# Eight decoded weight pieces and a gate table: their stores moved from SyncE's queue to GpSimd's

## The chip, the core and the metric

The program runs on one core of a Trainium2 chip. The metric is the time of one execution on the device in microseconds (us), the median of the executions shown. Three executions of the kernel before took 786.92, 788.0 and 788.8 us, so the median is 788.0 us. One more execution was profiled; all rows below are of that one.

## The reference

Three layers follow one another on 2304 tokens of width 512.

```
scores = scale * q @ k^T            # 4 batches, 8 heads, 576 positions, head width 64
attn   = softmax(where(mask, scores + bias, -1e9))     # causal, window 128, linear bias
x      = attn @ v                   # 2304 x 512
expert = argmax(x @ w_gate); gate = softmax(x @ w_gate)[expert]
out[t] = gate[t] * relu(x[t] @ w1[expert]) @ w2[expert]   # 8 experts, 512 -> 1024 -> 512
y      = relu(out @ w_in)**2 @ w_out                       # 512 -> 2048 -> 512
```

`w_in` and `w_out` reach the kernel as 64-bit words (two 32-bit words for each number), so they have to be decoded to 32-bit floats on the chip before they can be used. All large products are done on 16-bit floats with a high and a low half for each number, three products in place of one.

## The kernel before, in words

The program is one long, unrolled stream. A framework orders the instructions of every engine and adds the waits; each engine then runs its own instructions strictly in that order. The queue that an instruction stands in therefore matters twice: for what it waits for, and for what waits behind it.

**Stages.** Attention runs to about 160 us and writes its result, split into halves, to DRAM (`xd`, line 415, issued by GpSimd). The eight experts follow, to about 425 us, each in two steps: `s1` (lines 804 to 814: 96 matmuls into PSUM, a RELU on ScalarE at line 813, the low half on VectorE at line 814) and `s2` (lines 855 to 869: 96 matmuls, a copy on ScalarE at line 867). The last layer runs from about 438 us on (`wide1`, `wide2`).

**Expert weights.** `load_w` (line 761) loads a piece of 512 KB from DRAM through SyncE's queue (line 770) into a ring `rw` of four buffers, and splits it into halves on ScalarE (line 784) and VectorE (line 785). The buffer is free when line 785 is done.

**Expert inputs.** `gather` (line 997) fetches rows of `xd` with indirect DMAs from GpSimd's queue (line 793) into a ring `xg` of six buffers. A gather has to wait until TensorE has transposed what was in its buffer (line 801, `turn`), and while it waits, GpSimd's queue stands still.

**Weights of the last layer.** While the experts run, `wide()` (line 939) is called now and then and does one piece. `out_step` (line 920) takes one of the sixteen 128-row pieces of `w_out`. It loads 512 KB into the same ring `rw` (line 879), and three VectorE instructions decode it into the lower half of one tile `dec` (lines 884, 885, 886). Its `finish` (line 925), which the next `wide()` calls, splits it into halves on ScalarE (line 930) and VectorE (line 931). Eight of the sixteen pieces (`SENT`) are not kept on the chip: their halves go into the upper half of `dec`, and from there to DRAM (`wod`, 256 KB each, line 934). Since `dec` is one tile, line 930 of the next piece may not write before the store of this one has landed. Those eight are the first eight steps; the sixteen steps of `w_in` (`in_step`, line 889) follow, whose decoding uses the upper half of `dec` as well; `fetch_out` (line 970) brings `wod` back just before the last layer.

The store itself isn't issued by `finish`. It is put on a list (`self.stored`), and the next call of `wide()` issues it on SyncE's queue ahead of its own work, or after it when the next step is one of `w_in`.

**The gate table.** `gates()` (line 576) computes the gate of each token, transposes it into `gt` (line 596), and stores it to DRAM (`gd`) with eight small DMAs from SyncE's queue: four of 2 KB (line 600) and four of 0.25 KB (line 603). It is read again by indirect DMAs of GpSimd (line 757) from 284 us on.

In the rows below, the eight stores of `w_out` pieces are called p1 to p8 in the order of their issue.

Of the kernel before, what the change touches and what calls it, by code (L numbers as in the profile page):

```python
# [22 lines left out]
N, DM, E, F, F2 = 2304, 512, 8, 1024, 2048  # L23
P = 128
# [65 lines left out]
class K:  # L90
# [485 lines left out]
    def gates(self):  # L576

        nc, cp, V = self.nc, self.cp, self.nc.vector
        sh = [P, NT, E]
        G = cp.tile(sh, F32, name="G2")  # L580
        V.tensor_tensor(G, self.lg, self.mx[:, :, 0:1].to_broadcast(sh), op=ALU.subtract)
        nc.scalar.activation(G, G, AF.Exp, scale=1.0 / (XSC * GSC))
        gs = cp.tile([P, NT], F32, name="gs")
        V.tensor_reduce(gs, G, axis=AX.X, op=ALU.add)
        V.tensor_scalar(gs, gs, 1e-9, XSC * W1SC * W2SC, op0=ALU.add, op1=ALU.mult)

        self.gate = cp.tile([P, NT], F32, name="gate")
        g3 = gs.rearrange("p (g t) -> p g t", g=2)
        for g in range(2):
            V.reciprocal(self.gate[:, 8 * g:8 * g + 8].rearrange("p (b u) -> p b u", b=2),  # L590
                         g3[:, g, :8].rearrange("p (u b) -> p b u", b=2))
        V.reciprocal(self.gate[:, 16:], g3[:, :, 8])
        gp = self.psum("d", [P, P])[:NT]
        nc.tensor.transpose(gp, self.gate, self.idf)
        gt = cp.tile([NT, P], F32, name="gateT")
        V.tensor_copy(gt, gp)

        gd = self.gd.rearrange("(a r) o -> a (r o)", a=B)
        for a in range(B):
            nc.sync.dma_start(gd[a, :512].rearrange("(u p) -> u p", p=P), gt[4 * a:4 * a + 4])  # L600
        for a in range(B):
            o = a % 2 * 64
            nc.sync.dma_start(gd[a:a + 1, 512:], gt[16 + a // 2:17 + a // 2, o:o + 64])

    def order(self):

# [313 lines left out]
    def out_step(self, fc):  # L920

        nc = self.nc
        f = self.wide_load(self.wo, [(slice(fc * P, (fc + 1) * P), lambda r, k: r, DM, lambda st, k: st)])

        def finish():
            if fc in KEPT:
                dst = self.wo_s[fc]
            else:
                dst = self.dec[:, 512:].bitcast(F16).rearrange("p (a d) -> p a d", a=2)
            nc.scalar.activation(dst[:, 0], f, AF.Copy, scale=WOSC)  # L930
            nc.vector.scalar_tensor_tensor(dst[:, 1], f, WOSC, dst[:, 0], op0=ALU.mult, op1=ALU.subtract)  # L931
            if fc not in KEPT:
                o = SENT.index(fc) * 2 * DM
                self.stored.append(lambda: nc.sync.dma_start(self.wod[:, o:o + 2 * DM],
                                                             dst.rearrange("p a d -> p (a d)")))

        return finish

    def wide(self, k=1):
        def store():  # L940
            while self.stored:
                self.stored.pop()()

        for _ in range(k):
            store()
            if self.finish:
                self.finish()
                self.finish = None
            if self.steps:
                f, *a = self.steps.pop(0)  # L950
                if f == self.in_step:
                    store()
                self.finish = f(*a)

    def open_wide(self, stack):
        wp = self.wp = stack.enter_context(self.tc.tile_pool(name="wp", bufs=1))
        self.wi_s = [wp.tile([P, 2, 2, 7 * P], F16, name=f"wi{k}", tag=f"wi{k}") for k in range(8)]
        self.wo_s = {}
        self.stored, self.finish = [], None
        self.steps = [(self.out_step, fc) for fc in SENT] + \  # L960
            [(self.in_step, fp, kp) for fp in range(8) for kp in range(2)] + [(self.out_step, fc) for fc in KEPT]

# [13 lines left out]
    def experts(self, stack):  # L976
# [33 lines left out]
        gather(1)  # L1010
        self.places()
        wide(2)
        self.s2([w[2, 0, k] for k in range(4)], self.hte, 0, EB * P, lambda d: wide())
        xt = self.new_xf(P)
        self.transpose_whole(xgs[0][0], xt)
        self.offsets()
        for e in range(E):
# [13 lines left out]
            for fc in range(8):  # L1031
                ht = self.hts(e, W)[fc]
                if e == 0:
                    self.s1_whole(fc, w[1, e, fc // 2], xt, ht, W)
                else:
                    self.s1(fc, w[1, e, fc // 2], xt[:, :, :W], ht, W)
                hts.append(ht)
                if fc % 2 == 1 and more and e > 0:
                    w[1, e + 1, fc // 2] = self.load_w(1, e + 1, fc // 2)
                if fc in STEPS[e][0]:  # L1040
                    wide()
                if fc in (3, 5, 7) and more:
                    turn(nxt, e + 1, fc // 2 - 1)
                if e == 7 and fc == 1:
                    next(nrm)
                next(table, None) if table else None
# [283 lines left out]
```

## Time and profile before

| | |
|---|---|
| median of three executions | 788.0 us (786.92 to 788.8) |
| the profiled execution's own time | 787.16 us |
| its span, first to last instruction | 785.5 us |
| TensorE busy | 731.0 us (93%) |
| VectorE, ScalarE, GpSimd busy | 539.7, 362.6, 158.2 us |
| moved by SyncE's queue, by GpSimd's | 75.70 MB, 14.63 MB |

The span is 1.7 us shorter than the execution's own time, which holds what lies around the program. A busy share over the whole span hides that the stages differ: the last layer, from 440 us on, is nearly pure matmul work, and what idle time TensorE has lies before it. Rows of a timeline give start and duration in us, then engine, line, operation and tiles; in square brackets stands how long the engine was idle before the instruction and what ended that. SyncE's DMA instructions are issues: the transfer itself goes on after them, up to its landing.

### The profile page before, as it was taken

How to read it: one execution, taken by the hardware profiler on the slowest of the kernel's cores; microseconds unless marked ns; L12 is line 12 of the kernel's file. 1: busy time of each engine (PE TensorE's matmuls, PEld its weight loads, DVE VectorE, ACT ScalarE, POOL GpSimd, SP SyncE). 2: the span in 40 equal slices, each digit the busy share in tenths (PEclk: the TensorE clock that was granted, in tenths of full speed). 3: DMA queues.
4: the chain of work that ended last, by engine and by line, in shares of the span. 5: the costliest groups of instructions: out<-in, count | busy, mean ns of one | idle time of the engine just before them, and what ended most of it. 6: DMA issues, size and time to landing. Idle time of an engine off the chain costs nothing. (4 is left out here: it accounts for less than half of the span.)

```text
span 785.5 us, 18379 instructions
## 1 busy us (share of the span) xinstructions
PE 731.0 (93%) x7546; PEld 562.5 (72%) x7546; DVE 539.7 (69%) x1361; ACT 362.6 (46%) x637; POOL 158.2 (20%) x167
## 2 busy tenths in 40 slices
PE   6999999898878988998898999999999999999996
PEld 5889899687544654677698677777777777777772
DVE  5888888755679977878887865656656565657440
ACT  5888888634356554655643323232323232323220
POOL 4573212445101877100000000000000000000000
PEclk9999999998999999999999999999999999999999
DMA  9896307756686676765722200000000000000000
GB/s 335 299 359 142 98 29 211 207 121 204 215 248 219 195 222 202 239 199 180 252 82 61 78 15 14 15 15 15 15 15 15 15 15 14 16 3 27 2 28 28
DMA packets 36431, 91.54 MB, mean 117 GB/s; under 512 B 5992, under 2 KB 14200, under 8 KB 36344
## 3 DMA queue, kind: packets, MB, share of 16 engines
q1 hardware_dynamic: 29816, 75.70, 30.5%
q0 software_dynamic: 6528, 14.63, 5.9%
q8 instruction: 61, 1.00, 0.6%
q14 instruction: 26, 0.21, 0.1%
HBM read 77.44 MB, written 12.94 MB: 115 GB/s over the span
## 5 line engine op out<-in xcount | busy, mean ns | idle before, releaser
L1177 PEld LDWEIGHTS <-wi 128*128 128x128 f16 x3024 | 172.0, 98 | 4.0
L1238 POOL DMA_INDIRECT out_dram<-o,oid x18 | 17.5, 973 | 447.0 <-ACT o L1236 447.0
L1197 ACT CAST wr<-work 128x1024 f16<-128x1024 f32 x36 | 37.6, 1045 | 123.1 <-DVE work L1196 123.1
L784 ACT ACTIVATE wr<-rw 128x1024 f16<-128x1024 f32 x60 | 62.6, 1055 | 51.6 <-DMA rw<-in_w_dram 50.6
L785 DVE SCALAR_TENSOR_TENSOR wr<-rw,wr 128x1024 f16<-128x1024 f32 x60 | 72.6, 1219 | 18.7 <-ACT wr L784 18.6
L864 PE MATMUL ps_c<-work,wr 128*128 128x352 f16 (+5 forms) x256 | 72.8, 291 | 8.6 <-ACT yT L867 5.1
L865 PE MATMUL ps_c<-work,wr 128*128 128x352 f16 (+5 forms) x256 | 72.9, 291 | 8.2 <-DVE work L814 8.2
L866 PE MATMUL ps_c<-work,wr 128*128 128x352 f16 (+5 forms) x256 | 72.8, 291 | 0.0
L305 PE MATMUL ps_a<-yT,wr 128*128 128x192 f32 (+2 forms) x288 | 64.6, 345 | 6.2 <-DMA wr<-in_q_dram 4.5
L1202 DVE TENSOR_TENSOR work<-work 128x512 f32<-128x512 f32 x18 | 12.4, 691 | 77.5 <-ACT work L1189 77.5
L1177 PE MATMUL ps_a<-work,wi 128*128 128x128 f16 x1032 | 64.6, 219 | 0.0
L1177 PE MATMUL ps_c<-work,wi 128*128 128x128 f16 x1008 | 64.3, 221 | 0.0
L1177 PE MATMUL ps_b<-work,wi 128*128 128x128 f16 x984 | 62.1, 220 | 0.0
L317 ACT ACTIVATE pb<-pb,nm 128x192 f32<-128x192 f32 (+2 forms) x144 | 55.8, 432 | 12.0 <-DVE nm L310 11.8
L1229 PE MATMUL ps_d<-wr 128*128 128x512 f16 x144 | 54.6, 379 | 2.7 <-PEq L1076 2.7
L1230 PE MATMUL ps_d<-wr 128*128 128x512 f16 x144 | 54.6, 379 | 0.0
L1231 PE MATMUL ps_d<-wr 128*128 128x512 f16 x144 | 54.6, 379 | 0.0
L1231 PE MATMUL ps_d<-rw,wr 128*128 128x512 f16 x144 | 54.6, 379 | 0.0
L1230 PE MATMUL ps_d<-rw,wr 128*128 128x512 f16 x144 | 54.6, 379 | 0.0
L1229 PE MATMUL ps_d<-rw,wr 128*128 128x512 f16 x144 | 54.6, 379 | 0.0
L1231 PEld LDWEIGHTS <-wr 128*128 128x128 f16 x288 | 28.2, 98 | 33.9
L1229 PEld LDWEIGHTS <-wr 128*128 128x128 f16 x288 | 28.1, 98 | 33.3 <-issue 2.9
(261 smaller groups left out, 1691.5 us busy)
## 6 DMA issues: line engine op xcount, KB each, us to landing
rw<-in_w_dram SPq DMA_DIRECT2D x60, 512.0 KB, 5.1
rw<-in_wo_dram SPq DMA_DIRECT2D x16, 512.0 KB, 5.5
rw<-in_wi_dram SPq DMA_DIRECT2D x32, 256.0 KB, 4.1
wr<-in_q_dram SPq DMA_DIRECT2D x14, 512.0 KB, 18.1
xd<-xhl POOLq DMA_DIRECT2D x16, 256.0 KB, 6.6
yT<-in_k_dram SPq DMA_DIRECT2D x7, 576.0 KB, 7.6
rw<-in_v_dram SPq DMA_DIRECT2D x12, 325.0 KB, 5.6
wr<-in_q_dram SPq DMA_DIRECT2D x8, 256.0 KB, 6.5
```

The source lines that it names most:

```text
L305: nc.tensor.matmul(ps[:, s, first:hi], q[g, u, hh // 4][:, hh % 4, s if u < 4 else 0, :], self.kt[g, hh // 2][:, hh % 2, key0:key0 + hi - ...
L317: self.last_exp = nc.scalar.activation(pb[:, s, first:hi], pb[:, s, first:hi], AF.Exp, bias=nm[:, s:s + 1], scale=-1.0)
L784: self.nc.scalar.activation(t[:, 0], st, AF.Copy, scale=sc)
L785: self.nc.vector.scalar_tensor_tensor(t[:, 1], st, sc, t[:, 0], op0=ALU.mult, op1=ALU.subtract)
L864: nc.tensor.matmul(py, wh, hh, start=fc == 0, stop=False)
L865: nc.tensor.matmul(py, wh, hl, start=False, stop=False)
L866: nc.tensor.matmul(py, wl, hh, start=False, stop=fc == 7)
L1177: self.nc.tensor.matmul(ps[:, j], w[:, kp, a, w0 * P:(w0 + 1) * P], v[:, 2 * x + kp], start=kp + b == 0, stop=kp == 1 and b == 2)
L1197: nc.scalar.copy(g[0][:, :, i], ci)
L1229: nc.tensor.matmul(py, gh, wh, start=n == 0, stop=False)
L1230: nc.tensor.matmul(py, gh, wl, start=False, stop=False)
L1231: nc.tensor.matmul(py, gl, wh, start=False, stop=n == 15)
```

## The change

Both kinds of store are issued from GpSimd's queue, and that of a decoded piece at once in `finish`. The list of stores and the two places that emptied it are gone.

```diff
         gd = self.gd.rearrange("(a r) o -> a (r o)", a=B)
         for a in range(B):
-            nc.sync.dma_start(gd[a, :512].rearrange("(u p) -> u p", p=P), gt[4 * a:4 * a + 4])
+            nc.gpsimd.dma_start(gd[a, :512].rearrange("(u p) -> u p", p=P), gt[4 * a:4 * a + 4])
         for a in range(B):
             o = a % 2 * 64
-            nc.sync.dma_start(gd[a:a + 1, 512:], gt[16 + a // 2:17 + a // 2, o:o + 64])
+            nc.gpsimd.dma_start(gd[a:a + 1, 512:], gt[16 + a // 2:17 + a // 2, o:o + 64])
...
             if fc not in KEPT:
                 o = SENT.index(fc) * 2 * DM
-                self.stored.append(lambda: nc.sync.dma_start(self.wod[:, o:o + 2 * DM],
-                                                             dst.rearrange("p a d -> p (a d)")))
+                nc.gpsimd.dma_start(self.wod[:, o:o + 2 * DM], dst.rearrange("p a d -> p (a d)"))
...
     def wide(self, k=1):
-        def store():
-            while self.stored:
-                self.stored.pop()()
-
         for _ in range(k):
-            store()
             if self.finish:
                 self.finish()
                 self.finish = None
             if self.steps:
                 f, *a = self.steps.pop(0)
-                if f == self.in_step:
-                    store()
                 self.finish = f(*a)
...
-        self.stored, self.finish = [], None
+        self.finish = None
```

## Rows read from the trace of the kernel before

**Rows 1.** Busy time by stretch; columns: PE, PEld, DVE, ACT, POOL, PEclk, DMA share, GB/s

```profile
176.00:240.00 64.00, 50.66 (x397) 36.65 (x396) 39.84 (x68) 29.13 (x50) 15.78 (x19) 0.90 0.70 221
...
440.00:785.50 345.50, 339.22 (x3634) 237.09 (x3631) 199.30 (x295) 97.52 (x131) 17.51 (x18) 1.00 0.04 15
```

**Rows 2.** Waits of PE, 176 to 232 us: total, times, longest, in us

```profile
PE ps_c L865 <- DVE work L814: 3.3, 1, 3.3
...
PE ps_b L810 <- DVE work L814: 2.2, 1, 2.2
```

**Rows 3.** Timeline of DVE around 210 us

```profile
209.49 0.69 DVE L931 SCALAR_TENSOR_TENSOR dec<-dec 128x512 f16<-128x512 f32 x1
210.09 0.55 DVE L814 SCALAR_TENSOR_TENSOR work<-ps_b,work 128x384 f16<-128x384 f32 x1
```

**Rows 4.** Timeline of ACT, 187 to 216 us

```profile
187.97 0.63 ACT L930 ACTIVATE dec<-dec 128x512 f16<-128x512 f32 x1
...
193.57 0.63 ACT L930 ACTIVATE dec<-dec 128x512 f16<-128x512 f32 x1 [1.64 <-DMA wod<-dec]
...
200.18 0.63 ACT L930 ACTIVATE dec<-dec 128x512 f16<-128x512 f32 x1 [4.75 <-DMA wod<-dec]
...
203.80 0.63 ACT L930 ACTIVATE dec<-dec 128x512 f16<-128x512 f32 x1 [2.67 <-DMA wod<-dec]
...
207.26 1.06 ACT L784 ACTIVATE wr<-rw 128x1024 f16<-128x1024 f32 x1 [2.45 <-DMA rw<-in_w_dram]
...
208.59 0.62 ACT L930 ACTIVATE dec<-dec 128x512 f16<-128x512 f32 x1
...
215.98 0.61 ACT L930 ACTIVATE dec<-dec 128x512 f16<-128x512 f32 x1
```

**Rows 5.** Timeline of SyncE's queue, 183 to 211 us: p1 to p6 and one weight load

```profile
183.90 0.33 SPq L934 DMA_DIRECT2D wod<-dec  x1
...
189.35 0.33 SPq L934 DMA_DIRECT2D wod<-dec  x1
...
194.95 0.33 SPq L934 DMA_DIRECT2D wod<-dec  x1
...
201.56 0.33 SPq L934 DMA_DIRECT2D wod<-dec  x1
...
203.48 0.34 SPq L770 DMA_DIRECT2D rw<-in_w_dram  x1
...
205.19 0.35 SPq L934 DMA_DIRECT2D wod<-dec  x1
...
210.20 0.33 SPq L934 DMA_DIRECT2D wod<-dec  x1
```

**Rows 6.** The eight stores of line 934: duration of the issue (ns), and landing

```profile
L934 SPq DMA_DIRECT2D wod<-dec x8: 326/330/355, 183.9 to 223.9; - x8
...
DMA to landing us min/median/max: 2.1/3.7/5.4
```

**Rows 7.** Waits of SyncE's queue, 176 to 226 us: total, times, longest

```profile
SPq L934 <- DVE dec L931: 17.5, 7, 4.6
```

**Rows 8.** Line 415, two GpSimd stores at 141.9 and 142.5 us: landing

```profile
DMA to landing us min/median/max: 3.7/3.7/3.7
```

**Rows 9.** Line 793, nine GpSimd gathers from 176 to 200 us: landing

```profile
DMA to landing us min/median/max: 3.6/5.3/7.1
```

**Rows 10.** All DMA issues: GpSimd's 256 KB stores, median us to landing

```profile
xd<-xhl POOLq DMA_DIRECT2D x16, 256.0 KB, 6.6
```

**Rows 11.** Line 993, small plain DMAs of GpSimd: duration ns min/median/max

```profile
L993 POOL DMA_DIRECT2D ids<-ids x8: 555/764/810, 166.1 to 185.1; - x8
```

**Rows 12.** Timeline of GpSimd, 189 to 208 us

```profile
189.69 1.03 POOL L793 DMA_INDIRECT xg<-xd,idx  x1 [0.30 <-issue]
...
207.25 0.99 POOL L793 DMA_INDIRECT xg<-xd,idx  x1 [13.99 <-issue]
```

**Rows 13.** Instructions of line 884, 176 to 226 us: busy us, mean ns | idle before

```profile
L884 DVE TENSOR_SCALAR dec<-rw 128x512 uint32<-128x512 uint32 x8 | 3.4, 420 | 7.6 <-PE ps_c L866 7.5
```

## The prediction

> **What bounds the kernel now.** I read busy time by stretch first. From 440 us on TensorE works 339 of 345.5 us [rows 1]: nothing there can be gained or lost, except by starting earlier or later. In the 64 us in which the eight pieces are stored it works 50.7 us and idles 13.3 [rows 1], so a change to this stretch can move the time. The list of waits says what TensorE waits for there: two of its longest are for line 814 on VectorE, 2.2 us and 3.3 us [rows 2]. Line 814 needs little itself; in VectorE's order it stands behind line 931, the low half of a decoded piece [rows 3]. Line 931 comes straight after line 930 on ScalarE, and three of the line 930s waited for the landing of the store before: 1.64, 4.75 and 2.67 us [rows 4]. So in this stretch a chain goes round: store, landing, line 930, line 931, next store. It runs through the two engines that feed TensorE, and the time a store needs to land is a link of it. SyncE itself stood 17.5 us in front of stores that weren't ready yet [rows 7].
>
> **One round of the chain.** From line 930 to the store's issue it takes 1.38 us (193.57 to 194.95, 200.18 to 201.56, 203.80 to 205.19) [rows 4, 5]. From an issue to the next line 930 it took 4.07 us for p1, 4.22 for p2, 5.23 for p3, 2.24 for p4, 3.40 for p5 and 5.78 for p6 [rows 4, 5]. After p2, p3 and p4 it is the landing that ends the wait; after p1, p5 and p6 ScalarE wasn't idle, so other work (the decoding of the next piece, a weight load) came last.
>
> **What the change removes.** Sixteen issues leave SyncE's queue, 0.33 us each for the eight large ones [rows 6], and with them the 17.5 us of waiting [rows 7]. I cost this at nothing, and here is the cover: what stands behind a store is a load, and a load needs a ring buffer, which comes free when VectorE has decoded the next piece, and that comes after the same line 931 that the store waited for. The weight load at 203.48 shows it: the store ahead of it went at 201.56, and the load still waited 1.9 us [rows 5] for the decoding. If that cover were gone, a load could start up to those 1.9 us earlier.
>
> **What it adds.** GpSimd issues the eight large stores and the eight small ones.
>
> The small ones: no plain small DMA of GpSimd cost over 0.81 us, the median is 0.76 [rows 11], so eight take 6.1 us. Nothing on the chain waits for them, and GpSimd stands idle for 13.99 us before 207.25 [rows 12]. I take 0. If all eight stood in front of p5, that store would go some 5 us later; that is an upper end.
>
> The large ones: issue and landing change. For the start I add 0.3 us, the gap that GpSimd's queue shows between DMAs [rows 12]. The landing of a 256 KB store from GpSimd in this stretch isn't in the trace. Below, it can be no quicker than the quickest of the same stores from SyncE, 2.1 us [rows 6]. Above, the slowest gather of GpSimd in the stretch took 7.1 us [rows 9]; the 6.6 us median of all GpSimd's 256 KB stores [rows 10] lies inside. The row nearest in kind is the pair of GpSimd stores at 142 us, 3.7 us [rows 8]; the nearest in time is the median of the gathers, 5.3 us [rows 9]. I take the middle, 4.5 us, so that a round has 4.8 us from issue to the next line 930.
>
> **The walk.** With 4.8 in each place, and 1.38 to the next issue:
> - p1 at 183.90 gives a line 930 at 188.70, not 187.97: +0.7.
> - p2 at 190.08: 194.88, not 193.57: +1.3.
> - p3 at 196.26: 201.06, not 200.18: +0.9, since this one took 5.23 before.
> - p4 at 202.44: 207.24, not 203.80: +3.4, since this one took only 2.24.
> - p5 at 208.62: 213.42, not 208.59: +4.8.
> - p6 at 214.80: 219.60, not 215.98: +3.6 [rows 4, 5].
>
> On ScalarE part of p4's delay falls into the 2.45 us for which line 784 waits anyway [rows 4], but VectorE gets line 931, and line 814 behind it, late. TensorE's 2.2 us wait [rows 2, 3] then grows by about 4.8 us, and at the end of the stretch the whole stream is late by about 4. Afterwards nothing is timed from outside: each load waits for a buffer that VectorE frees. So I let the 4 us go through to the end: 787.16 + 4.0 = 791.2 for the profiled execution. That one lies 0.84 under the median, so against 788.0 the forecast is **792.0 us**.
>
> **The ends.** The same walk with 2.1 us to land ends about 4 us earlier than now: from p2 on the decoding and the loads come last. With 3.7 us it ends within half a microsecond of today; with 5.3 us it is 8.5 late, with 7.1 us 18 to 19. One microsecond of landing costs about 5 us, and break-even lies near 3.7.
>
> **A rule against the change.** Straight behind line 931, when GpSimd would write the descriptors, VectorE runs line 884, 0.42 us of TENSOR_SCALAR [rows 13]. The Trainium skill, "SBUF — State Buffer", section "Who interferes with whom", says that this kind can hold the port that GpSimd needs for writing descriptors, and that a DMA from SyncE doesn't depend on it. By that, as an estimate, a round would have 5.2 us and the walk would end 6 us late, at 794; no row here shows a GpSimd store held in this way, so the sum goes without it.
>
> **The rivals.**
> - **Faster (0.30): the stores land sooner.** Before, each store is queued with the 512 KB loads of SyncE; the quickest took 2.1 us and the slowest 5.4 [rows 6], a spread that a queue ahead would explain. If GpSimd's stores don't stand behind the loads, 2.1 to 2.5 us are possible, the waits of 1.64 and 4.75 us shrink, and the time is 788.0 − 3.5 = 784.5. It decides below 3.7 us. For it: the spread. Against it: GpSimd's own DMAs took 3.6 us at the least here [rows 9]. The Trainium skill, "DMA: Bandwidth & Descriptors", section "Queues, rings and completion order", states that an engine takes turns between queues, packet by packet, which would favour this rival.
> - **No difference (0.18).** The landing is near 3.7 us as at 142 us [rows 8]; p3 gains what p4 loses: 788.0.
> - **Parked (0.08).** GpSimd's queue is in order too, and its gather at 207.25 waits, through 13.99 us of idleness [rows 12], until TensorE has emptied its buffer. If p4 were put behind it, it would go at about 208.5, line 930 would come near 213.1 and not 203.80, and after p5 the stream would be some 10 us late: 798. For it: the order is the framework's, and the gather is free to stand before the store. Against it: p4 is issued 5.7 us before that gather now [rows 5, 12].
>
> **How the numbers follow.** The chain with slower landings gets 0.44, since of the three medians for GpSimd's landings two lie well above break-even and one on it [rows 8 to 10]; with the parked case 0.52 is slower. A measurement of this kernel can tell about 0.2%, 1.6 us. The likeliest case alone runs from 789 to 798. The range takes in the faster rival and lets landings reach 6.2 us (+14): 784 to 802. Left out is a lucky queue below and landings over 6.2 us above, some 2 in 10.
>
> **What would show it.** In the changed profile: landings of line 934's stores from GpSimd (4.5 us forecast, 3.7 the border); line 930's waits for them, now 9.06 us in three, at 15 or more in five or more; p8 some 4 us later than 223.9 [rows 6]; SyncE's waits for line 934 gone, with its loads still paced by VectorE; the last layer starting 4 us later and as long as before. I'm wrong if the stores land under 3.7 us, if another order of the queues takes the store off ScalarE's path, or if the 4 us are made good before 440 us.

## The result, and the profile of the changed kernel

The changed kernel is **slower**: 794.1 us (median of eight runs) against 787.5 us for the kernel before in the same comparison, ratio 1.0094 [1.0065, 1.0123], that is 5 to 10 us. Its profiled execution took 792.3 us with a span of 790.2 us, against 787.2 and 785.5. The forecast was 792.0 us in a range of 784 to 802, slower. The sign was right and the time lies near the middle of the range; the way there was another one, and the profile shows it.

Start with busy time by stretch of the changed kernel, columns as in [rows 1]; the middle row is used further down, with an experiment.

```profile
176.00:240.00 64.00, 50.14 (x401) 37.22 (x399) 37.75 (x65) 26.32 (x46) 25.25 (x37) 0.91 0.68 212
...
290.00:320.00 30.00, 24.62 (x153) 14.85 (x152) 21.90 (x39) 16.89 (x25) 23.91 (x21) 0.89 0.63 187
...
440.00:790.00 350.00, 341.62 (x3671) 239.47 (x3671) 203.25 (x305) 97.73 (x131) 17.50 (x18) 0.99 0.05 17
```

In the stretch of the stores VectorE does 2.1 us less work than before in the same 64 us, and ScalarE 2.8 us less: the work that feeds TensorE has fallen behind. From 440 us on the kernel has 4.5 us more to go than it had [rows 1]. Next, ScalarE's timeline, the rows that answer to [rows 4]; in brackets stands the idle time before an instruction and what ended it.

```profile
182.90 0.63 ACT L930 ACTIVATE dec<-dec 128x512 f16<-128x512 f32 x1
...
194.47 0.63 ACT L930 ACTIVATE dec<-dec 128x512 f16<-128x512 f32 x1 [7.24 <-DMA wod<-dec]
195.01 0.26 ACT L832 ACTIVATE work<-ps_a 128x128 f16<-128x128 f32 x1
...
198.55 0.63 ACT L930 ACTIVATE dec<-dec 128x512 f16<-128x512 f32 x1 [0.97 <-DMA wod<-dec]
...
203.73 0.63 ACT L930 ACTIVATE dec<-dec 128x512 f16<-128x512 f32 x1 [0.62 <-DMA wod<-dec]
...
208.00 0.63 ACT L930 ACTIVATE dec<-dec 128x512 f16<-128x512 f32 x1 [1.27 <-DMA wod<-dec]
...
212.77 0.63 ACT L930 ACTIVATE dec<-dec 128x512 f16<-128x512 f32 x1 [0.44 <-DMA wod<-dec]
...
218.62 0.63 ACT L930 ACTIVATE dec<-dec 128x512 f16<-128x512 f32 x1 [1.86 <-DMA wod<-dec]
...
225.10 0.62 ACT L930 ACTIVATE dec<-dec 128x512 f16<-128x512 f32 x1
```

One wait stands out. The second line 930 waited 7.24 us for the landing of the first store, p1; before it started at 187.97 without a wait [rows 4], now at 194.47. The other five waits are short, 5.16 us together. Why p1 landed so late is in the timeline of GpSimd, which now issues the stores.

```profile
183.70 1.76 POOL L991 TENSOR_SCALAR idx<-ids 128x3 uint32<-128x3 uint32 x4
185.52 0.81 POOL L985 DMA_DIRECT2D ids<-ids  x1
188.14 0.21 POOL L991 TENSOR_SCALAR idx<-ids 128x2 uint32<-128x2 uint32 x1 [1.82 <-DMA ids<-ids]
188.85 1.00 POOL L793 DMA_INDIRECT xg<-xd,idx  x1 [0.50 <-PE ps_b L831]
190.15 0.98 POOL L793 DMA_INDIRECT xg<-xd,idx  x1 [0.30 <-issue]
191.14 0.61 POOL L934 DMA_DIRECT2D wod<-dec  x1
196.12 0.56 POOL L934 DMA_DIRECT2D wod<-dec  x1 [4.37 <-DVE work L833]
...
200.21 0.58 POOL L934 DMA_DIRECT2D wod<-dec  x1 [0.91 <-DVE dec L931]
205.38 0.56 POOL L934 DMA_DIRECT2D wod<-dec  x1 [4.60 <-DVE dec L931]
206.03 2.03 POOL L600 DMA_DIRECT2D gd<-gateT  x4
208.05 1.51 POOL L603 DMA_DIRECT2D gd<-gateT  x3
209.65 0.56 POOL L934 DMA_DIRECT2D wod<-dec  x1
...
214.58 0.56 POOL L934 DMA_DIRECT2D wod<-dec  x1 [3.89 <-PE ps_a L812]
...
227.36 0.58 POOL L934 DMA_DIRECT2D wod<-dec  x1 [3.00 <-DVE dec L931]
```

p1's data were complete when line 931 ended on VectorE:

```profile
183.56 0.69 DVE L931 SCALAR_TENSOR_TENSOR dec<-dec 128x512 f16<-128x512 f32 x1 [3.90 <-ACT dec L930]
```

That is 184.25 us, and the store went at 191.14. For 6.9 us it stood in GpSimd's queue behind an index list's load and its landing (188.14), and behind two gathers (188.85 and 190.15), the first of which shows a wait of 0.50 us for TensorE. From SyncE p1 had gone at 183.90 [rows 5]. So p1 went 7.24 us later than before (191.14 against 183.90), and what came after it was *quicker* as a whole: from p1's issue to the seventh line 930 it is 27.48 us (191.14 to 218.62), where it was 32.08 [rows 4, 5]. TensorE paid at another place than foreseen:

```profile
PE ps_c L864 <- ACT work L832: 3.2, 1, 3.2
PE ps_c L865 <- DVE work L814: 3.0, 1, 3.0
PE ps_d L801 <- DMA xg<-xd,idx: 2.4, 1, 2.4
...
```

This is the list of its waits from 176 to 232 us, columns as in [rows 2]. The wait of 3.2 us is new: line 832 ran on ScalarE at 195.01, straight behind the line 930 that had waited 7.24 us. The 2.2 us wait in line 810 [rows 2] is gone. All waits of this list together came to 9.8 us before and come to 10.3 now, so TensorE pays only a small part of the loss in this window; between 240 and 440 us it then works another 1.9 us less (176.90 us, before 178.84).

The stores themselves, in the view of line 934 that answers to [rows 6]:

```profile
L934 POOL DMA_DIRECT2D wod<-dec x8: 558/570/623, 191.1 to 227.4; - x8
...
DMA to landing us min/median/max: 3.4/3.9/5.4
```

The landings in the last row are of the three stores for which the trace has one (p3, p6 and p8); for the others the next line 930 shows it. From issue to the next line 930, whose wait the landing ended each time, p1 to p6 took 3.33, 2.43, 3.52, 2.62, 3.12 and 4.04 us.

### The profile page after: what moved, and what is told of

It is laid out like the page before. It is cut to its first block, busy times and chain, and to the rows that moved or that the text cites. A ratio compares the mean times of both kernels' runs of the same rounds, so it can differ in the third digit from the quotient of the medians.

```text
span 790.2 us, 18382 instructions
## 1 busy us (share of the span) xinstructions
PE 731.8 (93%) x7546; PEld 562.5 (71%) x7546; DVE 541.1 (68%) x1361; ACT 362.4 (46%) x637; POOL 169.6 (21%) x183
## 3 DMA queue, kind: packets, MB, share of 16 engines
q1 hardware_dynamic: 28624, 73.59, 29.5%
## 5 line engine op out<-in xcount | busy, mean ns | idle before, releaser
L864 PE MATMUL ps_c<-work,wr 128*128 128x352 f16 (+5 forms) x256 | 75.1, 297 | 12.3 <-ACT yT L867 6.2
L865 PE MATMUL ps_c<-work,wr 128*128 128x352 f16 (+5 forms) x256 | 75.0, 296 | 10.0 <-DVE work L814 8.8
L866 PE MATMUL ps_c<-work,wr 128*128 128x352 f16 (+5 forms) x256 | 75.0, 296 | 0.0
## 6 DMA issues: line engine op xcount, KB each, us to landing
yT<-in_k_dram SPq DMA_DIRECT2D x7, 576.0 KB, 10.3
```

What stands on the lines that cost most here:

```text
L864: nc.tensor.matmul(py, wh, hh, start=fc == 0, stop=False)
L865: nc.tensor.matmul(py, wh, hl, start=False, stop=False)
L866: nc.tensor.matmul(py, wl, hh, start=False, stop=fc == 7)
```

## The experiments

The theory: the loss is the place of the first stores in GpSimd's queue, not the way in which GpSimd moves them. The main rival: GpSimd's stores cost something of their own, in issue or landing. Each ratio is against the kernel before on the same chip. Eight of the twelve runs were on chips where times spread more (all but the two of the first part and the two with p1 alone out of the way), and their intervals are wider.

**One part of the change alone.** First the gate table's eight small stores from GpSimd, in the kernel before:

```diff
-            nc.sync.dma_start(gd[a, :512]...
+            nc.gpsimd.dma_start(gd[a, :512]...
...
-            nc.sync.dma_start(gd[a:a + 1, 512:]...
+            nc.gpsimd.dma_start(gd[a:a + 1, 512:]...
```

> The kernel before, but with the eight stores of the gate table issued from GpSimd's queue; the stores of the decoded pieces stay as they were. Both theories: no difference, within 1.5 us, since nothing on the chain waits for them and GpSimd is idle there. If the small stores had a part in the loss: +1 us or more.

Ratio 1.0013 [0.9994, 1.0032]: no difference that can be told. In the changed kernel they take 0.5 us each on GpSimd and stand straight ahead of p5 (the rows of lines 600 and 603 in its timeline, seven of the eight), and still p5 went 1.65 us after its line 930 (208.00 to 209.65), like p2, p3 and p4.

Then p1 alone from GpSimd, in the kernel before:

```diff
-                self.stored.append(lambda: nc.sync.dma_start(self.wod[:, o:o + 2 * DM], ...))
+                if fc == SENT[0]:
+                    nc.gpsimd.dma_start(self.wod[:, o:o + 2 * DM], ...)
+                else:
+                    self.stored.append(lambda: nc.sync.dma_start(self.wod[:, o:o + 2 * DM], ...))
```

> The kernel before, but with p1 alone issued from GpSimd's queue; p2 to p8 and the gate table stay on SyncE's. Theory A: this one store brings most of the loss, +3 to +6 us against the kernel before. Theory B: one landing out of eight is longer by half a microsecond or so: +0.7 us, within what can't be told from no change.

Ratio 1.0028 [1.0004, 1.0052]: slower, by 2.2 us. The timeline of GpSimd shows the same picture; this profiled execution reached the stretch some 4 us late.

```profile
192.24 0.24 POOL L1002 TENSOR_SCALAR idx<-ids 128x2 uint32<-128x2 uint32 x1 [1.82 <-DMA ids<-ids]
192.95 1.00 POOL L793 DMA_INDIRECT xg<-xd,idx  x1 [0.47 <-issue]
194.25 0.98 POOL L793 DMA_INDIRECT xg<-xd,idx  x1 [0.30 <-issue]
195.23 0.61 POOL L935 DMA_DIRECT2D wod<-dec  x1
```

The line 930 that follows waited 6.28 us on ScalarE. Moving this one store of eight costs about a third of what the whole change costs (2.2 of 7.4 us by the ratios). That is under the 3 to 6 us expected: p1's place alone, with the other seven on SyncE, doesn't bring most of the loss.

**The first store out of the way.** In the changed kernel, p1 is put ahead of the third expert's last gather and of the later index work, once by an order on GpSimd's queue, once by taking p1 back to SyncE:

```diff
...
+            late = lambda c: tc.issue_after(self.p1.ins) if e >= 3 or e == 2 and c == 2 else ExitStack()
...
+                with late(c):
+                    xgs[e].append(self.gather_x(idx[:m, e, c:c + 1]))
```

> The changed kernel, but with the first store (p1) put ahead, in GpSimd's order, of the last gather of the third expert's inputs and of all index work and gathers behind it. Theory A (the loss comes from p1 standing behind two gathers on GpSimd's queue; the landings themselves are no slower than from SyncE): p1 is issued near 185 us and not at 191, the next line 930 starts near 188.5 and not at 194.5, and the time falls by 4 to 7 us against the changed kernel, to 786 to 789 us or a little less. Theory B, the forecast (every landing from GpSimd is longer): the rounds p2 to p8 still lose, and the time stays at 792 or above.

```diff
-                nc.gpsimd.dma_start(self.wod[:, o:o + 2 * DM], ...)
+                (nc.sync if fc == SENT[0] else nc.gpsimd).dma_start(self.wod[:, o:o + 2 * DM], ...)
```

> The changed kernel, but with p1 alone issued from SyncE's queue, at once; p2 to p8 and the gate table stay on GpSimd's. Theory A: 785 to 789 us, the whole loss gone, since only p1 was held up. Theory B: at most 1 us comes back, 793 us.

Ratios 1.0038 [1.0014, 1.0063] and 1.0055 [1.0023, 1.0087]. The first takes back more than half of the loss, and its interval lies just clear of the changed kernel's; with the second the middle value falls too, but the intervals overlap, and the 785 to 789 us that were expected of it didn't come (792.55 us in the median). What is left has the same form one store later. GpSimd in the kernel with p1 first:

```profile
185.25 0.60 POOL L934 DMA_DIRECT2D wod<-dec  x1 [0.72 <-PE ps_a L831]
...
190.03 1.02 POOL L793 DMA_INDIRECT xg<-xd,idx  x1 [0.30 <-issue]
191.94 0.37 POOL L996 TENSOR_SCALAR idx<-ids 128x2 uint32<-128x2 uint32 x1 [0.89 <-DMA ids<-ids]
192.44 0.62 POOL L934 DMA_DIRECT2D wod<-dec  x1
```

And with p1 on SyncE (there line 930 came at 187.74, and p2's data were ready some 1.4 us later):

```profile
188.45 0.71 POOL L991 TENSOR_SCALAR idx<-ids 128x2 uint32<-128x2 uint32 x1 [1.80 <-DMA ids<-ids]
189.44 1.06 POOL L793 DMA_INDIRECT xg<-xd,idx  x1 [0.28 <-issue]
190.80 0.99 POOL L793 DMA_INDIRECT xg<-xd,idx  x1 [0.30 <-issue]
191.79 0.61 POOL L934 DMA_DIRECT2D wod<-dec  x1
```

There p2 stands behind the very gathers that had stopped p1, landed 5.6 us after its issue, and the next line 930 waited 4.68 us. The stop had moved, not gone.

**The first two stores out of the way**, in the same two manners:

```diff
...
+                k = 0 if e == 2 and c == 2 else {3: 1}.get(e)
+                with tc.issue_after(self.sent[k].ins) if k is not None else ExitStack():
+                    xgs[e].append(self.gather_x(idx[:m, e, c:c + 1]))
```

> The changed kernel, with the first store put on GpSimd's queue ahead of the third expert's last gather, and the second store ahead of the fourth expert's gathers; every other gather stays where it was. Parking theory (the whole loss comes from these two stores standing behind gathers, for the landings are 2.3 to 3.9 us): the second store starts by 191.5 us against 196.1, and the time is that of the kernel before, ratio 0.998 to 1.003. Rival, GpSimd's stores cost something of their own wherever they stand (a landing, the issue, a port): at least half of the loss stays, 1.004 or more, with the second store early all the same.

```diff
-                nc.gpsimd.dma_start(self.wod[:, o:o + 2 * DM], ...)
+                (nc.sync if fc in SENT[:2] else nc.gpsimd).dma_start(self.wod[:, o:o + 2 * DM], ...)
```

> The changed kernel, with the first two stores on SyncE's queue and six on GpSimd's. Parking theory: no gather is moved and the two stores that would be parked are not on that queue; the time is that of the kernel before, ratio 0.998 to 1.003. Rival one, the parking only moves on to the third store, as it moved from the first to the second when the first alone was taken off: the third store starts 3 us or more after line 931, and the ratio stays near 1.005. Rival two, GpSimd's six landings cost by themselves: no store late, but 1.004 or more.

Ratios 1.0018 [0.9980, 1.0056] and 1.0011 [0.9974, 1.0049]. Both intervals hold 1 and end below the changed kernel's lowest bound, 1.0065. With all eight stores (the first) or six of them (the second) still on GpSimd's queue, no loss can be told; a rest of up to 0.5% isn't excluded. One number missed its expectation here: in the kernel with the order, p2 went at 192.37 and not by 191.5, 4.8 us after its line 930, since the index work ahead of it waited 2.84 us for its list; the next line 930 waited 3.00 us. So this kernel freed p1 and not yet p2, and even so no loss can be told. In the one with SyncE, p3 was the next to meet the gathers, but barely: the last one at 196.38, p3 at 197.58, 2.2 us after its line 930.

The profiles agree, as far as single executions can, in the stretch itself. In the kernel before it goes from p1's line 930 to p8's in 39.48 us:

```profile
182.47 0.63 ACT L930 ACTIVATE dec<-dec 128x512 f16<-128x512 f32 x1
...
221.95 0.61 ACT L930 ACTIVATE dec<-dec 128x512 f16<-128x512 f32 x1
```

The changed kernel takes 42.20 us for it and the one with p1 alone on GpSimd 44.23; with p1 out of the way it is 37.54 (by order) and 40.55 (by SyncE), with p1 and p2 38.51 and 38.70. The kernel with the gate table alone moved takes 38.06, so that a difference of 1.4 us says little. Lengths are compared because the first line 930 itself falls anywhere from 181.19 to 190.15 us in these profiles, a spread wider than the whole loss. So it is shown that the loss shrinks as the first stores leave their place behind the gathers; that this place is the whole of the loss isn't.

**Other queues.** Every store and the gate table back on SyncE, but issued at once and not one step later, as the kernel before does:

```diff
-                nc.gpsimd.dma_start(self.wod[:, o:o + 2 * DM], ...)
+                nc.sync.dma_start(self.wod[:, o:o + 2 * DM], ...)
```

> The changed kernel with every store and the gate table back on SyncE's queue, but issued at once, not one step later as in the kernel before: only the place in SyncE's order differs from before, for the load of the next piece now stands behind the store and so behind line 931. Parking theory read for SyncE: the load of the next piece goes out later by what line 931 needs, some 2 us for each of the pieces whose load was out early, and the time is 788 to 793, ratio 1.001 to 1.007. Rival, loads have room: the same as before, 0.998 to 1.002, and the later place of the store in the kernel before bought nothing.

Ratio 1.0008 [0.9963, 1.0053]: nearer to the rival of that text, no difference, though the interval takes in most of the other range too. The part of the change that drops the delayed issue costs nothing that shows. In SyncE's queue in this kernel the loads of line 879 still follow the stores by 2 to 3 us (182.62 and 185.66, 187.68 and 189.82, 191.86 and 193.78), waiting for their buffers.

The same from ScalarE's queue:

```diff
-                nc.gpsimd.dma_start(self.wod[:, o:o + 2 * DM], ...)
+                nc.scalar.dma_start(self.wod[:, o:o + 2 * DM], ...)
```

> The changed kernel, but with the eight stores of the pieces issued from ScalarE's queue: no gathers ahead of them and no weight loads either. Theory A: no parking, so 785 to 788 us, as before or a little less; what ScalarE loses is a wait of 0.7 us for line 931 and the issue, eight times, 2 us at most. Theory B: landings as short as from SyncE, so also as before. It tells neither theory from the other, but GpSimd's queue from the change of place in the order: if it stays at 792, the place and not the queue is the cost.

Ratio 1.0071 [1.0009, 1.0132], where 785 to 788 us were expected, as before or a little less. ScalarE's timeline shows no long stop at a landing:

```profile
202.52 0.33 ACTq L934 DMA_DIRECT2D wod<-dec  x1
205.34 0.63 ACT L930 ACTIVATE dec<-dec 128x512 f16<-128x512 f32 x1 [1.94 <-DMA wod<-dec]
206.72 0.33 ACTq L934 DMA_DIRECT2D wod<-dec  x1
```

Here an issue waits on ScalarE's own queue until line 931 is done, 1.38 us after line 930 started, and what stands behind it there waits too. But from the first line 930 to the eighth this execution takes 36.84 us, 2.6 us less than the kernel before, so its profile doesn't put the loss into this stretch. By that text's rule a time near 792 us charges the place in the order and not the queue; but with the same place on SyncE's queue, the run above, no loss shows. Where this kernel loses stays open, and the interval is wide.

**The loop cut.** If the landing's place in the chain is what counts, a piece that needn't wait for the store ahead of it should be faster from either queue. Each piece's halves are written into a w_in weight tile that isn't in use yet, instead of into the one scratch area:

```diff
-                dst = self.dec[:, 512:].bitcast(F16).rearrange("p (a d) -> p a d", a=2)
+                dst = self.wi_s[SENT.index(fc)].rearrange("p a b c -> p (a b c)")[:, :2 * DM].rearrange("p (a d) -> p a d", a=2)
```

In the kernel before, with SyncE's stores, two times:

> The kernel before, stores on SyncE's queue, but each piece's halves are written into a w_in tile that isn't used until 235 us or later, eight tiles for eight pieces, so that line 930 never waits for a landing. If the landing is a link of the chain that feeds TensorE: the waits of line 930 for wod (9.1 us) are gone, and the time falls by 2 to 4 us, to 783 to 785. If the chain then only waits for the decoding and the loads: no difference within 1.5 us.

> Once more the kernel before in which each piece's halves are written into a tile of the w_in weights that is not yet in use, so that line 930 never waits for a store to land. If the first answer (ratio 0.993) was right: 0.990 to 0.997, some 782 to 785 against 787. If it came from a noisy chip: 0.998 to 1.002, and the 9.06 us of waits in line 930 of the kernel before are made up for later in any case.

And in the changed kernel, with GpSimd's:

> The changed kernel, stores on GpSimd's queue, and the same eight tiles as sources. Neither a landing nor a place behind a gather can hold up line 930 now. If these two are all that the change costs: as fast as the kernel with the eight tiles and SyncE's stores, within 1.5 us, and faster than the changed kernel by 7 us or more. If GpSimd's queue costs in another way (its gathers late, VectorE or TensorE hindered): 2 us or more behind it.

With SyncE 0.9934 [0.9877, 0.9992] and 0.9936 [0.9890, 0.9983]: 5 us faster than the kernel before, twice, and the one version here that beats both kernels. In its second profile ScalarE no longer waits for a store anywhere in the stretch:

```profile
184.38 0.63 ACT L930 ACTIVATE wi<-dec 128x512 f16<-128x512 f32 x1
...
192.28 0.63 ACT L930 ACTIVATE wi<-dec 128x512 f16<-128x512 f32 x1 [0.33 <-issue]
...
196.65 0.63 ACT L930 ACTIVATE wi<-dec 128x512 f16<-128x512 f32 x1
...
213.86 0.63 ACT L930 ACTIVATE wi<-dec 128x512 f16<-128x512 f32 x1
```

The first and the last of these are the first and the eighth piece: 29.5 us, where the kernel before takes 39.5 and the changed kernel 42.2 (182.90 to 225.10). TensorE was busy for 56.66 of the 64 us from 176, not 50.66 [rows 1]. With GpSimd's stores the ratio is 1.0036 [0.9976, 1.0095], which can't be told from 1. p1 was again parked (it went at 193.11, its line 930 had run at 185.26), and nobody waited for it. Yet the middle value lies 8 us above that of the kernel with SyncE's stores, run beside it on the same chip, and the two intervals share only 0.9976 to 0.9992. So the expectation, as fast within 1.5 us, didn't come true; the other branch of its text, that GpSimd's queue costs in another way than through line 930, is the likelier one. The two profiled executions, 790.38 and 791.18 us, are too nearly alike to show what that way is. The main rival is thus not excluded as a part of the loss.

**Another miss.** More gathers were put behind stores, the third expert's last behind p2, the fourth's behind p4 and the fifth's behind p8:

```diff
...
+                k = 1 if e == 2 and c == 2 else {3: 3, 4: 7}.get(e)
+                with tc.issue_after(self.sent[k].ins) if k else ExitStack():
+                    xgs[e].append(self.gather_x(idx[:m, e, c:c + 1]))
```

> The changed kernel with all eight stores still on GpSimd's queue, but the gathers of that stretch put behind the stores that they could hold up: the last one of the third expert behind p2, those of the fourth behind p4, those of the fifth behind p8. Theory A (the loss is stores standing behind gathers): no store waits for a gather longer than 1 us, and the time is that of the kernel before or up to 3 us less, 784 to 788 us. Theory B (landings from GpSimd are longer): +2 us or more against the kernel before remains even so.

Ratio 1.0181 [1.0131, 1.0231], the slowest of all. The stores went well (186.3 to 224.4), but the kernel lost time later on, in a stretch where the changed kernel has the middle row of the first fence:

```profile
290.00:320.00 30.00, 18.01 (x61) 6.13 (x60) 12.12 (x20) 9.60 (x14) 19.92 (x19) 0.56 0.46 137
```

TensorE issued 61 matmuls in place of 153, at a granted clock of 0.56 in place of 0.89, and PE's waits there have no releaser but "issue": the profile names nothing that it waited for. Only the order on GpSimd differs from the changed kernel. Whether the later gathers cost this, or something that this view doesn't show, stays open; the kernel says nothing about the stores.

## Why the prediction came out right, and where it was wrong

**The chain: right.** Store, landing, line 930, line 931, next store is what times this stretch. Six of the changed kernel's seven rounds end with a wait for a landing, and cutting the chain there, with SyncE's stores, brings 5 us.

**The start: wrong, and this is the step that failed.** "For the start I add 0.3 us, the gap that GpSimd's queue shows between DMAs." For five of the six this held well: line 930 to issue took 1.65, 1.66, 1.65, 1.65 and 1.81 us for p2 to p6, against 1.38 to 1.61, so 1.28 us more over the five together. For p1 it was 8.24 us (182.90 to 191.14). The forecast weighed parking, with 0.08, but asked only of p4 and the gather at 207.25 whether a store would meet one. The rows to ask were of the same view of the kernel before, GpSimd's timeline, straight ahead of the first row of [rows 12]:

```profile
185.09 0.81 POOL L993 DMA_DIRECT2D ids<-ids  x1
187.68 0.27 POOL L999 TENSOR_SCALAR idx<-ids 128x2 uint32<-128x2 uint32 x1 [1.78 <-DMA ids<-ids]
188.39 1.00 POOL L793 DMA_INDIRECT xg<-xd,idx  x1 [0.44 <-issue]
```

An index list's load, the wait for it to land, and gathers up to 193 us: p1, ready at 184, and p2, ready at 189, fall into that. The term "+0.7" of p1 was +6.50 (line 930 at 194.47 against 187.97).

**The landing: mis-sized, in the other direction.** The walk took 4.8 us from issue to the next line 930; measured were 2.43 to 4.04, 19.06 us for the six together, against 24.94 before, 5.88 us less. Five of the six are below the 3.7 us that the prediction named as the border, so by its own sign it was wrong on this. In the three rounds that the landing ended in both kernels (p2 to p4) 3.12 of the 5.88 us came back, as the faster rival said; in the other three ScalarE's other work came last before, and how much of their 2.76 us is landing isn't shown. By the forecast's own walk the kernel would have been faster, had p1 not been late; the runs with p1 and p2 out of the way don't show that gain (1.0018 and 1.0011). The Trainium skill, "DMA: Bandwidth & Descriptors", section "Queues, rings and completion order", states that an engine takes turns between queues. By that such stores could land sooner than behind SyncE's loads, and the shorter rounds agree with it, but no run here shows that this is the cause, and p2's 5.6 us in the kernel with p1 on SyncE don't fit it. (The walk's "about 5 us" for a microsecond of landing is 6 above its break-even: it has six rounds.)

The sum of the stretch, from p1's issue to the seventh line 930: +7.24 for p1's start (0.43 of it already there at p1's own line 930, 182.90 against 182.47), +1.28 for the others' starts, −5.88 from issue to line 930, +2.64 us (218.62 against 215.98). The walk had +3.6 there, out of terms most of which were wrong: a start too small by 6.5 us and landings that were too long went against each other. That the number came out is luck.

**The rule on the port: not seen.** A store's issue on GpSimd took 558 to 623 ns: p1's, with no line 884 beside it, 607, and p2's, beside one that ran from 195.94 to 196.36 us, 565. Line 884 itself took 423 ns on average against 420 [rows 13]. The 6 us that the prediction worked out for such a hold would have needed longer rounds, and they were shorter. The Trainium skill, "SBUF — State Buffer", section "Who interferes with whom", says that this kind of instruction can hold the port; no run here shows that it did.

**What was costed at nothing: held.** The gate table (0.9994 to 1.0032 by itself), and SyncE's relief. Its waits for line 934 are gone as said, and VectorE still paces its loads; the list of SyncE's waits from 176 to 226 us, as in [rows 7]:

```profile
SPq L879 <- DVE work L833: 17.9, 2, 10.5
SPq L879 <- DVE dec L886: 12.3, 2, 8.9
...
```

**That the loss goes through to the end: right, but it grows on the way.** p8 went at 227.36, 3.4 us after the 223.9 of [rows 6]; the last decoded piece, further on, has its line 930 at 439.33 us in the changed kernel and at 435.33 in the kernel before, 4.0 us apart, and the span ends 4.7 us later. Of these 4.7 us the sum above holds 2.64; where the other 2.1 came in isn't shown. The runs' difference is larger than the profiles' (6.6 against 5.2 us), since the profiled run was the fastest of its eight.

Of the signs that were named, three came true (p8 about 4 us late, SyncE's waits gone, the last layer 4 us later); the landings of 4.5 us didn't, and line 930's waits came to 12.40 us, not to 15 or more, and 7.24 of that in one of six.

## What to carry to other kernels

Before an issue is moved to another engine's queue, write down for each instance what stands ahead of it there and what that waits for, for the first instance above all: a queue in order gives an instruction the delay of its neighbours, and here one store of eight, parked for 6.9 us behind an index list's load and two gathers, cost more time in the stretch than the shorter rounds gave back. When the cause is found, look one instance further, since the stop moved from p1 to p2 when p1 alone was taken away. And a landing that sits in a loop through a single buffer is better taken out by another buffer, here one that is still free, than shortened: that was worth 5 us with SyncE's stores, where the choice of the queue lost 7. Last, the length of a stretch tells more of a single profile than the moment at which it starts, and a time that comes out as forecast doesn't show that its terms did.

## What wasn't expected of the hardware

In the changed kernel the 256 KB stores of this stretch landed no later from GpSimd's queue than from SyncE's before: the line 930 that waited for them came 2.43 to 4.04 us after the issue, with SyncE 4.22, 5.23 and 2.24 in the three that ended a wait [rows 4, 5], with ScalarE 2.82 in the pair shown above. The 6.6 us median of GpSimd's other 256 KB stores [rows 10] was a bad guide for them. But the landing isn't one figure: p8's took 5.4 us, as long as the longest with SyncE [rows 6], and in the kernel with p1 on SyncE p2's took 5.6 us from GpSimd's queue. The gate table's small DMAs took 0.5 us each on GpSimd, below the 0.56 us that was the least of the index lists' loads [rows 11].
